# A planner of hand-scheduled steps that repeats its plan, feeds its waits back and counts all DMAs as one pipe

## The chip, the core and the metric

The program runs on one core of a Trainium2 chip. The metric is device time in microseconds (us) from the first to the last instruction, plus a little that lies around that span; the time given is a median of several executions, and a profile is taken of one execution.

## What is computed

Causal attention over two batches of 12 heads (448 positions, head size 64) gives x of 896 rows by 768. Two feed-forward stages follow, and only these are touched by the change:

```python
def _moe_ref(x, w_in, w_out):            # first feed-forward
    h = x @ w_in                         # 896x768 @ 768x2048
    g = h * np.cos(h)
    return (g @ w_out).astype(np.float32)   # 896x2048 @ 2048x768
...
def _moe2_ref(x, w_in, w_out):           # second feed-forward
    h = x @ w_in
    g = np.where(pos, h, np.where(neg, 0.0, (h + beta) ** 2 / (4.0 * beta)))
    return (g @ w_out).astype(np.float32)
```

The weights come as 64-bit floats and are decoded to 32-bit on the core.

## The kernel before

**Stages.** Attention comes first, in an order fixed by a table. Each feed-forward then has a first half (x @ w_in, matmuls of line L645, a few of L517) and a second half (g @ w_out, matmuls of L815). Every product of 32-bit values is made of three matmuls, since both operands are split into a high and a low part: the high part is a cast on ScalarE (ACT), the low part a subtraction on VectorE (DVE).

**The second half uses a seven-product scheme** (fewer block products, more sums): 28 products, numbered t = 0 to 27, seven groups of four, each of three pieces of six matmuls. Before product t its weight side (`wh`, `wl`) and its activation side (`xh`, `xl`) are split. The sums of blocks that the scheme needs are made partly by DMA: an accumulating DMA that POOL issues (L605), called S2, S3, S4 for weights (tile `ws`, 384 KB) and T2, T3, T4 for activations (tile `gs`, 448 KB), each with the block number 0 to 3 behind a dot.

**Loads.** The SP queue issues the weight loads in order: `raw` (L223, w_in, 768 KB in pieces of 1 KB) and `rows` (L730, w_out, 768 KB in pieces of 6 KB). There are two `raw` buffers, shared with the last `rows` of each stage, so the first two loads of the second feed-forward, raw16 and raw17, wait until DVE has decoded the `rows` that lie in their buffers.

**The planner.** All steps of both feed-forwards are registered with `plan.add(name, engine, us, make, after)`: a step's engine, its assumed duration, the function that emits its instructions, and the steps it must follow. Names begin with the stage, 0 or 1. The steps that matter here: `L` load a raw unit, `A` decode it on ACT (L241 and L243, two instructions), `l`, `a`, `k`, `m` the load of a `rows` unit, its words on ACT, its clamp and its bits on DVE (L246, then L262 and L265), `g` a sign change on POOL (L748), `wh`/`xh` the high parts on ACT (L773, L775), `wl`/`xl` the low parts on DVE (L781, L783), `N` a sign change on ACT (L602), `p1` a copy of a finished result bank on ACT (L827), `c` a sum of results on DVE (L838), `D` the products on TensorE (PE, L815).

`Plan.run` gives every step a latest start (`late`), counted back from the PE steps, whose order is fixed. Then it walks through time: each engine takes, of the steps that are ready, the one with the earliest `late`. A step's result counts as usable after a fixed lag, which for anything on SP is 6 us and on POOL 7 us however many DMAs are under way. The order found is the order in which the instructions are emitted, so each engine runs its own queue in that order, and an instruction that waits holds all behind it on its engine.

Of the kernel before, what the change touches and what calls it, by code (L numbers as in the profile page):

```python
# [88 lines left out]
class Plan:  # L89


    LAG = {"PE": 0.1, "ACT": 0.15, "DVE": 0.1, "SP": 6.0, "POOL": 7.0}

    MARGIN = 0.0
# [6 lines left out]
    def add(self, name, engine, us, make, after=(), lag=None):  # L101
        after = [(a, self.ops[a]["lag"]) for a in after if a in self.ops]
        op = dict(engine=engine, us=us, make=make, after=after, lag=self.LAG[engine] if lag is None else lag)
        if engine == "PE":
            if self.last_pe:
                op["after"].append((self.last_pe, 0.0))
            self.last_pe = name
        assert name not in self.ops
        self.ops[name] = op

    def run(self):

        ops = self.ops
        t = self.BUSY["PE"]
        for op in ops.values():
            op["late"] = 1e9
            if op["engine"] == "PE":
                op["late"] = t
                t += op["us"]
        order = list(ops)  # L120
        for name in reversed(self.sorted(order)):
            op = ops[name]
            for a, lag in op["after"]:
                margin = self.MARGIN if op["engine"] == "PE" and ops[a]["engine"] != "PE" else 0.0
                ops[a]["late"] = min(ops[a]["late"], op["late"] - lag - margin - ops[a]["us"])
        free = {e: self.BUSY.get(e, 0.0) for e in self.LAG}
        waiting = {e: [n for n in order if ops[n]["engine"] == e] for e in free}
        self.log = []
        while any(waiting.values()):
            best = None  # L130
            for e, names in waiting.items():
                can = []
                for n in names:
                    if all("end" in ops[a] for a, _ in ops[n]["after"]):
                        r = max([ops[a]["end"] + lag for a, lag in ops[n]["after"]] + [-9.0])
                        can.append((r, n))
                    if e == "PE":
                        break
                if can:
                    start = max(free[e], min(r for r, _ in can))  # L140
                    if best is None or start < best[0]:
                        ready = [n for r, n in can if r <= start]
                        best = (start, e, min(ready, key=lambda n: ops[n]["late"]))
            start, e, n = best
            waiting[e].remove(n)
            ops[n]["start"], ops[n]["end"] = start, start + ops[n]["us"]
            free[e] = ops[n]["end"]
            self.log.append((start, e, n, ops[n]["late"]))
            ops[n]["make"]()

    def sorted(self, order):
        seen, out = set(), []

        def visit(n):
            if n not in seen:
                seen.add(n)
                for a, _ in self.ops[n]["after"]:
                    visit(a)
                out.append(n)

        for n in order:
            visit(n)
        return out

# [2 lines left out]
def attention_then_two_ffn(  # L167
# [436 lines left out]
    def sum_by_dma(to, what):  # L604
        nc.gpsimd.dma_start(out=to, in_=what, accum_op=ALU.add)  # L605
# [11 lines left out]
    OWN = 10  # L617
# [3 lines left out]
    def ffn(k):  # L621
# [5 lines left out]
        XRING, P1, P17, P174 = ((0, 4, 5, 14), (BIG, 14, 5, 4))[k]  # L627
        x = x1 if k == 0 else None

        def add(name, engine, us, make, after=(), lag=None):  # L630
            plan.add(f"{k}{name}", engine, us, make, [a[1:] if a[0] == "@" else f"{k}{a}" for a in after], lag)

        def before(name):
            return ["@0" + name] if k else []
# [224 lines left out]
        def weights(f):  # L859
            u = base + f  # L860
            if (k, f) != (0, 2):
                add(f"A{f}", "ACT", 1.8, partial(decode, u), [f"L{f}"] + ([f"O{f - 2}"] if f > 1 else before(f"O{KF - 2 + f}")))
            add(f"K{f}", "DVE", 0.56, partial(decode, u), [f"A{f}"])
            add(f"M{f}", "DVE", 1.92, partial(decode, u), [f"K{f}"])
            if f + 2 < KF:
                add(f"L{f + 2}", "SP", 0.1, partial(load_unit, u + 2), [f"M{f}", f"L{f + 1}"])
            prior = [f"H{f - 1}"] if f else before(f"wh{NT7 - 1}")
            prior += unit_products(f - 4) if f >= 4 else [a for d in range(ML) for a in before(f"D{NT7 - 4 + f}.{d}")]
            add(f"H{f}", "ACT", 0.82, partial(decode, u), [f"M{f}"] + prior)
            if u in UNIT_LO_BY_DMA:  # L870
                add(f"h{f}", "ACT", 0.82, partial(decode, u), [f"H{f}"])
                add(f"O{f}", "POOL", 1.0, partial(decode, u), [f"h{f}"])
            else:
                add(f"O{f}", "DVE", 0.95, partial(decode, u), [f"H{f}"])

        if k:
            for f in range(2):
                add(f"L{f}", "SP", 0.1, partial(load_unit, base + f), [f"@0m{KF - 2 + f}"] + ([f"L{f - 1}"] if f else []))
            weights(0)
            weights(1)  # L880
        ACC = 0.6045
# [23 lines left out]
        for f in range(0, KF, 2):  # L905
# [14 lines left out]
            for i in (f, f + 1):  # L920
                j, ii, q = spot(i)
                need = unit_products(i) + ([f"X{i - 2}"] if i > 1 else [f"@0c12.{d}" for d in range(ML)] if k else [])
                if k == 0:
                    add(f"G{i}", "ACT", 1.85, partial(start_gate, i), need)
                    add(f"R{i}", "DVE", 1.05, step(gates, i), [f"G{i}"])
                    add(f"S{i}", "ACT", 1.15, step(gates, i), [f"R{i}"])
                    add(f"X{i}", "DVE", 1.05, step(gates, i), [f"S{i}"])
                else:
                    add(f"G{i}", "ACT", 2.95, partial(start_gate, i), need)
                    add(f"X{i}", "DVE", 1.1, step(gates, i), [f"G{i}"])  # L930
                    add(f"N{i}", "ACT", 0.55, step(gates, i), [f"X{i}"])
                if q and ii:
                    add(
                        f"T3.{j}", "POOL", 1.0, partial(lambda j: sum_by_dma(part(j, 1), part(j, 3)), j),
                        [f"X{i - 3}", f"X{i - 2}", f"X{i - 1}", f"X{i}", f"N{i}", f"N{i - 2}"],
                    )
                if i + 2 < KF:
                    weights(i + 2)
# [3 lines left out]
        for n in range(KF):  # L942
# [5 lines left out]
            add(f"l{n}", "SP", 0.1, partial(load_rows, n), ([f"l{n - 1}"] if n else []) + free + ([f"L{KF - 1}"] if n >= OWN else []))  # L948
# [3 lines left out]
            add(f"g{n}", "POOL", 0.65, partial(rows_minus, n), [f"m{n}"], lag=0.15)  # L952
            if i and not q:
                add(f"S3.{j}", "POOL", 1.0, partial(sum_by_dma, ws[j][:, 1], ws[j][:, 0]), [f"g{n - 1}", f"g{n}"])

        def ready_of(n):
            return f"m{n}", f"g{n}"
# [12 lines left out]
        def add_split(t):  # L970
# [6 lines left out]
            add(f"wh{t}", "ACT", 0.82, partial(split_hi, t, "w"), sw + ([f"wh{t - 1}"] if t else []) + [f"H{KF - 1}"] + done(t - 4))  # L977
            if t in by_dma:
                add(f"wm{t}", "ACT", 0.82, partial(split_lo_minus, t), [f"wh{t}"])
                add(f"wl{t}", "POOL", 1.0, partial(split_lo_add, t), [f"wm{t}"])  # L980
# [15 lines left out]
        for t in range(NT7):  # L996
# [12 lines left out]
                        need = [f"{a}{e}" for a in ("wh", "wl", "xh", "xl")] + (free[d // 2] if free else [])  # L1009
                        add(f"D{e}.{d}", "PE", 1.21, partial(product, e, d), need)  # L1010
            if p == 0:
                add(
                    f"T2.{j}", "POOL", 1.0, partial(lambda j: sum_by_dma(part(j, 0), part(j, 1)), j),
                    [f"T3.{j}", f"xh{t}", f"xl{t}"],
                )
            if p == 1:
                add(
                    f"S2.{j}", "POOL", 1.0, partial(sum_by_dma, ws[j][:, 1], ws[j][:, 3]),
                    [f"S3.{j}", f"wh{t}", f"wl{t}"] + odd(j),
                )  # L1020
                add(
# [5 lines left out]
                    [f"S2.{j}", f"wh{t - NJ}", f"wl{t - NJ}"],  # L1027
                )
            if p == 2:
                add(  # L1030
                    f"T4.{j}", "POOL", 1.0, partial(lambda j: sum_by_dma(part(j, 2), part(j, 0)), j),
                    [f"T2.{j}", f"xh{t}", f"xl{t}"],
                )
                add(
                    f"S4.{j}", "POOL", 1.0, partial(sum_by_dma, ws[j][:, 2], ws[j][:, 1]),
                    [f"S2.{j}", f"wh{t}", f"wl{t}"],
                )
            if j == NJ - 1:
# [62 lines left out]
```

## Time and profile before

| | us |
|---|---|
| median of 3 runs | 532.63 (532.59 to 533.18) |
| the profiled execution's own time | 532.24 |
| its span, first to last instruction | 530.4 |
| PE busy in the span | 517.1 (97%) |
| DVE busy | 432.8 (82%) |
| ACT busy | 396.5 (75%) |
| POOL busy | 120.3 (23%) |

The profiled execution lies 0.39 us under the median, and 1.84 us of its time lie around its span. "Idle" of an engine is the time in which it ran no instruction; the profile names what ended each idle stretch.

### The profile page before, as it was taken

To read this page: it belongs to the slowest core of one execution; us is meant where nothing else is said; L and a number is where in the kernel's file an instruction comes from. 1 tells how busy PE (TensorE), PEld (TensorE's weight loads), DVE (VectorE), ACT (ScalarE), POOL (GpSimd) and SP (SyncE) were. 2 spreads that over 40 slices of the span, in tenths; PEclk is the share of its full clock that TensorE was granted. 3 is DMA by queue.
4 is the path that set the end of the run, shared out by engine and by line. 5 is a ranking of instruction groups with operands and counts; after the bars stand their busy time and mean duration, and the time that the engine had idled before them with its cause. 6 is when DMAs were issued, how large, how long until landed. Compare 5 with 4: busy or idle time off the path is not lost.

```text
span 530.4 us, 7822 instructions
## 1 busy us (share of the span) xinstructions
PE 517.1 (97%) x2865; PEld 451.3 (85%) x2865; DVE 432.8 (82%) x589; ACT 396.5 (75%) x634; POOL 120.3 (23%) x178
## 2 busy tenths in 40 slices
PE   7999999999999999997999999999999999999996
PEld 3677668898989899896989999898989898999996
DVE  6878797999998989993997896879887489986751
ACT  5999856998988869862845677999989998655430
POOL 2766562203111112460000001011101235400000
PEclk9999999999999999999999999999999999999999
DMA  8741116957787346999030258577863779960111
GB/s 313 261 122 41 41 61 210 303 173 210 246 244 230 91 122 142 210 210 231 1 107 13 74 175 258 179 208 234 225 197 82 160 140 231 197 138 0 53 52 53
DMA packets 43702, 82.68 MB, mean 156 GB/s; under 512 B 2576, under 2 KB 31888, under 8 KB 43664
## 3 DMA queue, kind: packets, MB, share of 16 engines
q1 hardware_dynamic: 36464, 61.40, 35.4%
q0 software_dynamic: 6912, 20.45, 20.8%
q8 instruction: 22, 0.36, 0.3%
q10 hardware_dynamic: 288, 0.34, 0.2%
q14 instruction: 16, 0.13, 0.1%
HBM read 58.98 MB, written 2.75 MB: 116 GB/s over the span
## 4 chain that ended last, share of the span: by engine, by line
PE 85%; DVE 7%; DMA 4%; ACT 3%; issue 1%; DVEq 0%; ACTq 0%
PE m L645 41%; PE m L815 30%; PE o L466 4%; DMA raw<-in_moe_w_in 4%; PE m L517 2%; PE sa L352 2%; PE tx L441 2%; PE sb L352 1%; DVE s L781 1%; DVE slo L781 1%; PE sc L337 1%; PE tw L441 1%; PE warm L545 1%; PE tz L441 1%; DVE nma L380 1%
## 5 line engine op out<-in xcount | busy, mean ns | idle before, releaser
L645 PE MATMUL m<-x,whi 128*128 128x512 f32 (+2 forms) x728 | 204.8, 362 | 0.0
L815 PE MATMUL m<-s,shi 128*128 128x448 f32 x648 | 185.6, 368 | 4.2 <-ACT shi L773 3.3
L645 PEld LDWEIGHTS m<-x,whi 128*128 128x128 f32 x728 | 134.4, 188 | 14.2
L815 PEld LDWEIGHTS m<-s,shi 128*128 128x128 f32 x648 | 122.2, 189 | 15.4 <-ACT shi L773 3.7
L645 PE MATMUL m<-x,wlo 128*128 128x512 f32 (+2 forms) x364 | 131.9, 362 | 0.0
L815 PE MATMUL m<-s,slo 128*128 128x448 f32 x324 | 119.0, 367 | 0.0
L748 POOL TENSOR_SCALAR ws<-ws 128x384 f32<-128x384 f32 x32 | 25.9, 811 | 236.6 <-DVE ws L265 121.7
L645 PEld LDWEIGHTS m<-x,wlo 128*128 128x128 f32 x364 | 68.3, 188 | 7.0
L815 PEld LDWEIGHTS m<-s,slo 128*128 128x128 f32 x324 | 61.2, 189 | 5.4 <-DVE slo L781 0.5
L781 DVE TENSOR_TENSOR slo<-ws,shi 128x768 fp32r<-128x768 f32 x56 | 54.0, 967 | 9.5 <-ACT shi L773 9.5
L773 ACT CAST shi<-ws 128x768 fp32r<-128x768 f32 x56 | 46.1, 827 | 2.1 <-issue 1.8
L775 ACT ACTIVATE s<-gs 128x896 fp32r<-128x896 f32 x30 | 28.5, 948 | 19.1 <-PE m L815 15.5
L241 ACT ACTIVATE f<-raw 128x768 f32<-128x768 f32 x32 | 28.9, 906 | 15.0 <-DMA raw<-in_moe_w_in 13.7
L783 DVE SCALAR_TENSOR_TENSOR s<-gs,s 128x896 fp32r<-128x896 f32 x30 | 33.2, 1107 | 6.9 <-ACT s L775 6.8
L773 ACT CAST s<-gs 128x896 fp32r<-128x896 f32 x24 | 22.7, 945 | 20.4 <-PE m L815 20.3
L716 DVE TENSOR_TENSOR gs<-m,ax 128x896 f32<-128x896 f32 x16 | 17.5, 1091 | 22.6 <-ACT ax L714 18.8
L605 POOL DMA_DIRECT2D gs<-gs x24 | 23.3, 972 | 48.9 <-DVE s L783 14.1
L781 DVE TENSOR_TENSOR s<-gs,s 128x896 fp32r<-128x896 f32 x24 | 26.4, 1100 | 7.2 <-ACT s L773 7.1
L265 DVE SCALAR_TENSOR_TENSOR ws<-ws,rows 128x768 uint32<-128x768 uint32 x32 | 30.9, 964 | 1.1
L296 DVE TENSOR_TENSOR wlo<-f,whi 128x768 fp32r<-128x768 f32 x30 | 28.8, 960 | 3.4 <-ACT whi L287 3.4
L241 ACT ACTIVATE ws<-rows 128x768 f32<-128x768 f32 x32 | 29.1, 911 | 2.8 <-DMA rows<-in_moe_w_out 2.6
L262 DVE SCALAR_TENSOR_TENSOR rows<-rows 128x768 uint32<-128x768 uint32 x32 | 30.5, 953 | 0.3 <-ACT rows L243 0.2
(104 smaller groups left out, 799.9 us busy)
## 6 DMA issues: line engine op xcount, KB each, us to landing
raw<-in_moe_w_in SPq DMA_DIRECT2D x32, 768.0 KB, 4.7
rows<-in_moe_w_out SPq DMA_DIRECT2D x32, 768.0 KB, 5.2
gs<-gs POOLq DMA_DIRECT2D x24, 448.0 KB, 5.7
ws<-ws POOLq DMA_DIRECT2D x24, 384.0 KB, 6.9
v<-in_v SPq DMA_DIRECT2D x12, 256.0 KB, 2.7
k<-in_k SPq DMA_DIRECT2D x12, 224.0 KB, 3.9
qr<-in_q SPq DMA_DIRECT2D x11, 224.0 KB, 4.4
out<-c SPq DMA_DIRECT2D x11, 224.0 KB, 2.0
```

What stands on the lines that cost most here:

```text
L241: nc.scalar.activation(out=fl, in_=high.bitcast(F32), func=AF.Abs, scale=UP)
L262: nc.vector.scalar_tensor_tensor(out=low, in0=high, scalar=0x80000000, in1=low, op0=ALU.bitwise_and, op1=ALU.bitwise_or,)
L265: nc.vector.scalar_tensor_tensor(out=bits, in0=bits, scalar=3, in1=low, op0=ALU.logical_shift_left, op1=ALU.bitwise_or,)
L296: e.tensor_tensor(out=lo[:, :m], in0=fl, in1=f32(hi)[:, :m], op=ALU.subtract)
L605: nc.gpsimd.dma_start(out=to, in_=what, accum_op=ALU.add)
L645: nc.tensor.matmul(o, w[a][:, c, :], x_of(t, c)[:, s], start=(c == first and n == 0), stop=(c == last and n == 2),)
L748: nc.gpsimd.tensor_scalar(out=t, in0=t, scalar1=-1.0, scalar2=1.0, op0=ALU.mult, op1=ALU.mult)
L773: nc.scalar.copy(out=hi, in_=src)
L775: nc.scalar.mul(out=hi, in_=src, mul=-1.0)
L781: nc.vector.tensor_tensor(out=lo, in0=src, in1=f32(hi), op=ALU.subtract)
L783: nc.vector.scalar_tensor_tensor(out=lo, in0=src, scalar=-1.0, in1=f32(hi), op0=ALU.mult, op1=ALU.subtract)
L815: nc.tensor.matmul(o, l[:, i, d * P : (d + 1) * P], r[:, i], start=(p in (0, 2, 4) and j == 0 and i == 0 and n == 0), stop=(j == NJ - 1 an ...
```

## The change

Only the planner and the way in which steps describe their DMAs change. No step is added or removed and no dependency changes, so the same instructions run. The PE order is fixed, as before.

- A step that issues a DMA (`add_load`, `add_sum`) now carries the DMA's share of one common pipe (2.4 us for a load, 2.3 us for a sum). In the model DMAs leave this pipe one after the other, a DMA lands 2.6 us after it left, and a step is not issued while the pipe is more than 3 us behind.
- Durations of ACT, DVE and POOL steps are raised by 1.5 to 2%.
- `run` now plans up to 200 times. Of the best plan so far it picks one wait of PE, follows it back through what it waited for, and either makes the steps on the way more urgent (`early`) or holds one step back (`held`); a plan that ends no later is kept.

```diff
-    LAG = {"PE": 0.1, "ACT": 0.15, "DVE": 0.1, "SP": 6.0, "POOL": 7.0}
+    LAG = {"PE": 0.1, "ACT": 0.15, "DVE": 0.1, "SP": 0.1, "POOL": 0.15}
+    PACE = {"PE": 1.0, "ACT": 1.015, "DVE": 1.015, "SP": 1.0, "POOL": 1.02}
+    DMA_PACE = 1.1
+    LANDING = 2.6
+    BACKLOG = 3.0
     BUSY = {"PE": 11.8, "DVE": 1.3, "ACT": 1.5, "POOL": 0.6}
+    ROUNDS = 200
...
+    def once(self, early, held):
...
+                ready = [(max(r, pipe - self.BACKLOG) if ops[n]["dma"] else r, n, why) for r, why, n in steps]
...
+            r, n, why = min((x for x in ready if x[0] <= start), key=lambda x: ops[x[1]]["late"] - early.get(x[1], 0.0))
...
+            if op["dma"]:
+                pipe = end = max(pipe, free[e]) + op["pipe"]
...
+    def run(self):
+        self.wanted()
+        draw = random.Random(1)
+        early, held, best = {}, {}, None
+        for _ in range(self.ROUNDS):
+            end, log, waits, behind = self.once(early, held)
+            if best is None or end <= best[0]:
+                best = (end, log, waits, behind, early, held)
+            end, log, waits, behind, early, held = best
+            if not waits:
+                break
+            early, held = dict(early), dict(held)
+            wait, n = draw.choice(waits)
+            step = (wait + 1.0) * draw.uniform(-0.5, 3.0)
+            hold = draw.random() < 0.5
+            for _ in range(draw.randrange(1, 16)):
+                r, n, before = behind[n]
+                if n is None:
+                    break
+                if not hold:
+                    early[n] = early.get(n, 0.0) + step
+            if hold and n and behind[n][2]:
+                held[behind[n][2]] = behind[n][0]
+        self.log = best[1]
+        for _, _, n, _ in self.log:
+            self.ops[n]["make"]()
...
+        def add_load(name, make, after):
+            add(name, "SP", 0.1, make, after, 2.4)
+
+        def add_sum(name, make, after):
+            add(name, "POOL", 1.0, make, after, 2.3)
...
-                add(f"L{f + 2}", "SP", 0.1, partial(load_unit, u + 2), [f"M{f}", f"L{f + 1}"])
+                add_load(f"L{f + 2}", partial(load_unit, u + 2), [f"M{f}", f"L{f + 1}"])
```

**What moves.** The order differs in many places on ACT, DVE and POOL and in a few on SP. Three of them are shown, the rows of before first and those of the change behind (line numbers of the change are some 64 to 70 higher).

POOL, second half of the first feed-forward, from the sum S2.2 (tile ws2) to the last sum S4.3 (ws3); a `gs..0` that writes gs0..1 is a T4:

```order
L605 DMA ws2_1378<-ws2_1378 128x768
L605 DMA gs001_1461<-gs000_1435 128x896
L605 DMA ws0_1376<-ws0_1376 128x768
L605 DMA gs011_1708<-gs010_1677 128x896
L605 DMA ws1_1377<-ws1_1377 128x768
L605 DMA gs021_1956<-gs020_1929 128x896
L748 TENSOR_SCALAR ws3_1379<-ws3_1379 128x384
L605 DMA ws2_1378<-ws2_1378 128x768
L748 TENSOR_SCALAR ws3_1379<-ws3_1379 128x384
L605 DMA ws3_1379<-ws3_1379 128x768
L605 DMA gs031_2196<-gs030_2161 128x896
L605 DMA ws3_1379<-ws3_1379 128x768
```

```order
L669 DMA ws2_1378<-ws2_1378 128x768
L669 DMA gs001_1470<-gs000_1435 128x896
L669 DMA gs011_1709<-gs010_1673 128x896
L669 DMA ws0_1376<-ws0_1376 128x768
L818 TENSOR_SCALAR ws3_1379<-ws3_1379 128x384
L669 DMA gs021_1948<-gs020_1914 128x896
L818 TENSOR_SCALAR ws3_1379<-ws3_1379 128x384
L669 DMA gs031_2193<-gs030_2156 128x896
L669 DMA ws3_1379<-ws3_1379 128x768
L669 DMA ws1_1377<-ws1_1377 128x768
L669 DMA ws2_1378<-ws2_1378 128x768
L669 DMA ws3_1379<-ws3_1379 128x768
```

The sums S4.1 (ws1) and S4.2 (ws2) stood before the second sign change (g15) and now stand behind it, after T4.3 and S2.3.

DVE, the same stretch, around the decoding of rows014, which frees the buffer that raw16 is loaded into (`slo` is a `wl`, `s` an `xl`, `L246 ... ws3` a `k`):

```order
L781 TENSOR_TENSOR slo08_2463<-ws0_1376,shi08_2462 128x768
L781 TENSOR_TENSOR s09_2494<-gs011_1708,s09_2494 128x896
L781 TENSOR_TENSOR slo09_2505<-ws1_1377,shi09_2504 128x768
L246 TENSOR_SCALAR ws3_1379<-ws3_1379 128x2x384
L781 TENSOR_TENSOR s010_2522<-gs021_1956,s010_2522 128x896
L262 SCALAR_TENSOR_TENSOR rows014_2427<-rows014_2427 128x768
L265 SCALAR_TENSOR_TENSOR ws3_1379<-ws3_1379,rows014_2427 128x2x384
```

```order
L851 TENSOR_TENSOR slo08_2468<-ws0_1376,shi08_2467 128x768
L672 TENSOR_TENSOR ws0_1376<-ws0_1376 128x768
L310 TENSOR_SCALAR ws3_1379<-ws3_1379 128x2x384
L851 TENSOR_TENSOR s09_2502<-gs011_1709,s09_2502 128x896
L851 TENSOR_TENSOR slo09_2507<-ws1_1377,shi09_2506 128x768
L326 SCALAR_TENSOR_TENSOR rows014_2421<-rows014_2421 128x768
L329 SCALAR_TENSOR_TENSOR ws3_1379<-ws3_1379,rows014_2421 128x2x384
```

The clamp of rows014 now stands ahead of xl9 and wl9, and its bits directly behind wl9, ahead of xl10; a sum on DVE (S1.0) has moved ahead of it.

On ACT the decoding of raw16 (f16, step 1A0) stays where it was, between wh12 and wh13; that of raw17 moves from behind wh14 to behind wh16.

ACT, second half of the second feed-forward, from the split xh4 (`s14`) on; `gs131_...<-gs131_...` is a sign change, the last one N15, on which the sum T3.3 (to gs130) waits, and `p11` are the copies `p1`:

```order
L775 ACTIVATE s14_4148<-gs100_3255 128x896
L773 CAST shi14_4157<-ws0_1376 128x768
L602 ACTIVATE gs131_4001<-gs131_4001 128x448
L241 ACTIVATE ws2_1378<-rows112_3974 128x2x384
L243 ACTIVATE rows112_3974<-rows112_3974 128x768
L775 ACTIVATE s15_4186<-gs110_3487 128x896
L773 CAST shi15_4197<-ws1_1377 128x768
L827 COPY p11_4200<-m37_4089 128x448
L775 ACTIVATE s16_4208<-gs120_3730 128x896
L827 COPY p11_4200<-m37_4089 128x448
```

```order
L845 ACTIVATE s14_4155<-gs100_3256 128x896
L843 CAST shi14_4164<-ws0_1376 128x768
L666 ACTIVATE gs121_3760<-gs121_3760 128x448
L845 ACTIVATE s15_4177<-gs110_3486 128x896
L843 CAST shi15_4187<-ws1_1377 128x768
L897 COPY p11_4198<-m37_4084 128x448
L666 ACTIVATE gs131_3997<-gs131_3997 128x448
L897 COPY p11_4198<-m37_4084 128x448
L666 ACTIVATE gs131_3997<-gs131_3997 128x448
L897 COPY p11_4198<-m38_4085 128x448
```

N15 stood two splits ahead of `p1.0` and now follows `p1.1`.

## Rows read from the trace of the kernel before

**Rows 1.** Waits of PE from 95 us on: who waited, total us, times, longest us

```profile
PE m L815 <- ACT shi L773: 3.3, 1, 3.3
PE m L815 <- DVE c L838: 0.4, 1, 0.4
PE m L815 <- ACT p L827: 0.4, 2, 0.2
```

**Rows 2.** Timeline of PE where product 13 begins: start, us, what, idle before

```profile
250.86 1.11 PE L815 MATMUL m<-s,shi 128*128 128x448 f32 x2 [3.31 <-ACT shi L773]
```

**Rows 3.** Timeline of ACT, 237 to 250 us

```profile
248.44 0.89 ACT L241 ACTIVATE f<-raw 128x768 f32<-128x768 f32 x1 [9.66 <-DMA raw<-in_moe_w_in]
```

**Rows 4.** The chain that ended last: start, us, what

```profile
199.38 12.41 PE m L815 x60
...
229.71 18.70 DMA raw<-in_moe_w_in
...
308.12 115.66 PE m L645 x576
423.79 13.39 PE m L815 x66
...
438.62 87.84 PE m L815 x432
```

**Rows 5.** Stretch: us, busy PE PEld DVE ACT POOL, PEclk, DMA share, GB/s

```profile
247.00:256.00 9.00, 5.69 (x20) 4.49 (x19) 4.59 (x6) 7.56 (x10) 0.85 (x1) 0.81 0.49 127
```

**Rows 6.** DMA queues from 234 to 246 us: packets, MB, share of 16 engines

```profile
q0 software_dynamic: 673, 1.98, 85.0%
q1 hardware_dynamic: 737, 0.75, 22.1%
```

**Rows 7.** DMA queues and issues from 74 to 79 us, no sum under way

```profile
q1 hardware_dynamic: 784, 0.79, 50.9%
...
raw<-in_moe_w_in SPq DMA_DIRECT2D x2, 768.0 KB, 4.6
```

**Rows 8.** Timeline of POOL, sums issued around raw16's load

```profile
223.25 0.86 POOL L605 DMA_DIRECT2D ws<-ws  x1 [0.30 <-POOL ws L748]
...
228.07 0.86 POOL L605 DMA_DIRECT2D gs<-gs  x1 [0.44 <-DVE s L781]
...
230.83 0.86 POOL L605 DMA_DIRECT2D ws<-ws  x1
234.12 1.28 POOL L748 TENSOR_SCALAR ws<-ws 128x384 f32<-128x384 f32 x1 [2.43 <-DVE ws L265]
235.70 0.88 POOL L605 DMA_DIRECT2D ws<-ws  x1 [0.30 <-POOL ws L748]
236.27 1.18 POOL L605 DMA_DIRECT2D gs<-gs  x1
```

**Rows 9.** DMA issues from 223.2 to 223.3 us: KB each, us to landing

```profile
ws<-ws POOLq DMA_DIRECT2D x1, 384.0 KB, 6.9
```

**Rows 10.** DMA issues from 228 to 229 us

```profile
gs<-gs POOLq DMA_DIRECT2D x1, 448.0 KB, 13.9
```

**Rows 11.** Timeline of DVE, 224 to 230 us

```profile
224.16 1.09 DVE L781 TENSOR_TENSOR s<-gs,s 128x896 fp32r<-128x896 f32 x1 [0.40 <-ACT s L773]
...
226.04 0.55 DVE L246 TENSOR_SCALAR ws<-ws 128x768 f32<-128x768 f32 x1
...
227.69 0.95 DVE L262 SCALAR_TENSOR_TENSOR rows<-rows 128x768 uint32<-128x768 uint32 x1
```

**Rows 12.** Waits of PE before 95 us

```profile
PE sb L352 <- ACT p L402: 1.5, 2, 1.4
```

**Rows 13.** Timeline of ACT, second feed-forward: p1.1 and xh7

```profile
438.06 0.51 ACT L827 COPY p<-m 128x448 f32<-128x448 f32 x1
...
441.27 0.94 ACT L775 ACTIVATE s<-gs 128x896 fp32r<-128x896 f32 x1
```

**Rows 14.** DMA issues from 447 to 468 us

```profile
gs<-gs POOLq DMA_DIRECT2D x4, 448.0 KB, 8.9
```

More of the change, by code (lines that the diff above doesn't have):

```diff
@@ L1 @@
 import math
+import random
 import struct
@@ L109, in add, with lag, wanted @@
         self.ops[name] = op
-    def run(self):
-        ops = self.ops
+    def lag(self, a, op):
+        return 0.0 if a["engine"] == op["engine"] == "PE" else a["lag"]
+    def wanted(self):
         t = self.BUSY["PE"]
-        for op in ops.values():
+        for op in self.ops.values():
             op["late"] = 1e9
@@ L118, in run @@
                 op["late"] = t
[L119 to L125, printed above, removed]
+                t += op["time"]
+        for name in reversed(self.sorted()):
+            op = self.ops[name]
+            for a in (self.ops[n] for n in op["after"]):
+                a["late"] = min(a["late"], op["late"] - self.lag(a, op) - a["pipe"] - a["time"])
@@ L126, in run @@
+    def once(self, early, held):
+        ops = self.ops
+        need = {n: len(op["after"]) for n, op in ops.items()}
+        then = {n: [] for n in ops}
+        for n, op in ops.items():
+            for a in op["after"]:
+                then[a].append(n)
+        can = {e: [] for e in self.LAG}
+        for n in need:
+            if not need[n]:
+                can[ops[n]["engine"]].append((-9.0, None, n))
         free = {e: self.BUSY.get(e, 0.0) for e in self.LAG}
-        waiting = {e: [n for n in order if ops[n]["engine"] == e] for e in free}
@@ L128, in run @@
-        self.log = []
-        while any(waiting.values()):
+        last = dict.fromkeys(free)
+        pipe = 0.0
+        done, behind, log, waits = {}, {}, [], []
+        while len(log) < len(ops):
             best = None
[L131 to L149, printed above, removed]
@@ L151, in sorted @@
-    def sorted(self, order):
+            for e, steps in can.items():
+                if not steps:
+                    continue
+                ready = [(max(r, pipe - self.BACKLOG) if ops[n]["dma"] else r, n, why) for r, why, n in steps]
+                start = max(free[e], min(ready)[0])
+                if best is None or start < best[0]:
+                    best = (start, e, ready)
+            start, e, ready = best
+            r, n, why = min((x for x in ready if x[0] <= start), key=lambda x: ops[x[1]]["late"] - early.get(x[1], 0.0))
@@ new lines, in once @@
+            op = ops[n]
+            can[e] = [x for x in can[e] if x[2] != n]
+            behind[n] = (r, why, last[e])
+            last[e] = n
+            if e == "PE" and start > free[e]:
+                waits.append((start - free[e], n))
+            free[e] = start + op["time"]
+            end = free[e]
+            if op["dma"]:
+                pipe = end = max(pipe, free[e]) + op["pipe"]
+            done[n] = end
+            log.append((start, e, n, op["late"]))
+            for m in then[n]:
+                need[m] -= 1
+                if not need[m]:
+                    r, why = max((done[a] + self.lag(ops[a], ops[m]), a) for a in ops[m]["after"])
+                    can[ops[m]["engine"]].append((max(r, held.get(m, r)), why, m))
@@ L152, in sorted @@
+    def sorted(self):
         seen, out = set(), []
@@ L156, in visit @@
                 seen.add(n)
-                for a, _ in self.ops[n]["after"]:
+                for a in self.ops[n]["after"]:
                     visit(a)
                 out.append(n)
-        for n in order:
+        for n in self.ops:
             visit(n)
```

44 lines of the change are left out of this document (21 added, 23 removed).

## The prediction

> **What bounds the kernel now.** The page gives PE 97% of the span, and no step's work changes, so the first view to read is who made PE wait. From the end of attention on there are three kinds of wait: one of 3.3 us for the cast `shi` on ACT, two of 0.2 us for the copies `p`, one of 0.4 us for a sum `c` [rows 1]. The long one stands at 247.55 to 250.86 us, where product 13 of the first feed-forward should begin [rows 2]. The reader should next ask why ACT was late with that cast. It had no work of its own to finish: it sat idle for 9.66 us, until 248.44, in front of the decoding of raw16, and wh13 is queued right behind that decoding [rows 3]. The chain of waits names the same culprit, a load issued at 229.71 that took 18.70 us [rows 4], where the same kind of load takes 4.6 us when no sum is under way [rows 7].
>
> Why so long? While PE ran up to the stop, the queue of the sums moved 673 packets and the queue of the loads 737 in the same 12 us [rows 6]. The two queues take turns about packet by packet. A raw load consists of 784 packets [rows 7], small ones (1 KB pieces), and each waits for a far larger packet of a sum. At 737 per 12 us, 784 packets take 12.8 us; the other 5.9 us of the 18.70 lie before its first packet and behind its last. So the load is slow for as long as sums are queued.
>
> How much is there to win? Both feed-forwards run the same 504 matmuls of L815. The first does so from 199.38 to 308.12, in 108.74 us; the second from 423.79 to 438.62 + 87.84 = 526.46, in 102.67 us [rows 4]. The first loses 6.07 us more than the second. Each also has one wait of 0.2 us for `p` [rows 1], so waits in the products cost 6.07 + 0.4 = 6.5 us in all. Of these, 3.3 and 0.4 are the named idle times, and 1.7 is the clock: over the 9.00 us from 247 the granted clock is 0.81 on average, that is 2 x 0.19 x 9.00 = 3.4 us at 1.2 instead of 2.4 GHz, half of it lost [rows 5]. It fell after PE had stood still for 3.31 us. The rest, 0.7 us, I put to restarts. Everything else on PE is matmuls back to back, and the change neither shortens nor removes one.
>
> **The change part by part.** Nothing is added or removed; the planner runs before the program is built and costs nothing on the chip. The larger durations and the pipe in its model cost nothing by themselves either, they only pick the order. The price of the change is therefore what the new order does to the 6.5 us, and whether it makes a new wait.
>
> First, the load of raw16. It waits for the bits of rows014 on DVE. Those now follow wl9 directly. In the trace xl9 starts at 224.16, since it waits for ACT (0.40 us idle), then comes wl9, then the clamp at 226.04, one more split, and the bits at 227.69 [rows 11]. With the clamp and that split out of the way the bits can start at 226.04, 1.65 us earlier. (The clamp and S1.0 must then fit ahead of 224.16; T1.1, a sum of some 1.1 us on DVE, was moved behind, which makes the room.) So the load is issued 1.65 us earlier, near 228.1.
>
> Second, the sums around it. From 223.25 to 228.07 POOL issued six, which stood ahead of the load, one more at 230.83, and the next at 235.70 and 236.27, behind a sign change that ends at 235.40 [rows 8]. The first of the six landed at 223.25 + 6.9 = 230.15 [rows 9], the sixth at 228.07 + 13.9 = 241.97 [rows 10]: 2.36 us for each of the five between. In the new order S4.1 and S4.2 leave this place and go behind the sign change, T4.3 and S2.3. Five sums stand ahead of the load, and the last of them, T4.2, should land near 239.6. T4.3 is held by the sign change until about 235.4, so by these rows it joins some 4 us before the queue is empty, and the load keeps taking turns with sums to its end, as before.
>
> Third, what follows. If the load takes as long as it did, it lands 1.65 us earlier, and so does everything queued behind it on ACT (wh13, then wl13 on DVE). PE itself arrives 0.2 us earlier, without its first wait for `p`. The stop at product 13 shrinks from 3.31 to 3.31 - 1.65 + 0.2 = 1.9 us. Whether the clock falls after 1.9 us is not in the trace. It was kept after 1.4 us in attention [rows 12] and lost after 3.31; 1.9 is nearer to the first, so I take 0, and 1.7 as the upper end.
>
> Fourth, the two waits for `p` and that for `c`. The first two come from work that ACT does between the copies p1.0 and p1.1, a decoding in the first feed-forward, the split xh6 in the second; the decoding now stands ahead of both, and a shorter sign change has taken the split's place. The third was DVE's lateness after the long stop, which shrinks. I count all three as gone; 0.8 us is what they cost if none is.
>
> Fifth, the many other moves (sums and sign changes later in the second feed-forward, loads one or two places up or down). Their cover is the lead with which splits run ahead of PE; I cost them at nothing and take the tightest as a rival below.
>
> Sum: without any wait in the products, 532.24 - 6.5 for the profiled execution, 526.1 against the median of 532.63, which lies 0.39 us above. With 1.9 us left at product 13: **528.0 us**.
>
> **The rivals.** *No stop at all.* The sum S2.2 is held by a sign change behind the bits of rows013, and these move ahead of four DVE steps (two `wl`, an `xl` and the sum T1.1, each of about 1 us, as the steps of [rows 11]), so the five sums may start up to some 4 us earlier, and T4.2's packets may be through when T4.3 arrives near 235.4. Then raw16's packets have the pipe to themselves, 784 in 4.6 us instead of 12.8 [rows 7]. The stop vanishes if the load lands 1.9 us sooner than I forecast. For it speaks that a gap of 1 us moves about a fifth of the load, against it the 4 us of queue by the rows above. Time 526.1.
>
> The Trainium skill, page "DMA: Bandwidth & Descriptors", section "Queues, rings and completion order", says that an engine goes round its queues and takes some 9 to 17 descriptors from one before it switches. By that rule a raw load would pass in a few turns, the stop would not be there, and the time would come out as this rival's, 526.1. The trace does not agree: 673 packets to 737 in the same stretch [rows 6] are turns of about one to one, so the page adds little to this rival's chance.
>
> *The change does not do what it says there.* The pipe is full until all sums of this stretch are through, and as many bytes are asked for as before. If raw16 gets through only at the end of that crowd, it lands as late as before, the stop stays at 3.5 us and the clock falls. Then only the small waits go, 0.8 us: 531.8.
>
> *Slower.* In the second feed-forward T3.3 now waits for N15 behind `p1.1`. That copy ends at 438.57, and a sign change is short (the xh beside it takes 0.94), so T3.3 is issued near 439.1. Product 7 begins three products after 438.62: 54 matmuls of 87.84 / 432 = 0.203 us [rows 4], at 449.6. Ahead of it lie xh7, 0.94 us [rows 13], and xl7, 1.09 us [rows 11]. T3.3 may thus take 8.4 us. In the crowd of that stage such sums took 8.9 us [rows 14], but few stand ahead of T3.3. If it takes 13.9 us, as one did in the first feed-forward [rows 10], PE stops for 5.5 us there and loses 1.7 of clock: 535.2. It makes the kernel slower, on top of my forecast, from a landing of about 12.4 us on.
>
> **How the numbers follow.** Forecast, a shortened stop: 0.43, of which 0.13 with a fallen clock (529.7). No stop: 0.37. As late as before: 0.12. Slower: 0.08. A run of this kernel can tell about 0.2% from no change, 1.1 us. The first two cases are faster, and a little of the third: 0.85. The rest of the third and mild forms of the fourth are within 0.2%: 0.09. Slower: 0.06. The range reaches from the no-stop case less the uncertainty of the restarts (526.1 - 0.7 = 525.4) to a stop left at its full 3.3 us with the clock's 1.7 us (526.1 + 5.0 = 531.1), which leaves out the last two cases.
>
> **What would show it.** Right: the wait of PE for the cast `shi` at product 13 is 1 to 3 us; ACT's idle time in front of raw16's decoding is shorter than 9.66 us but still the longest; the load is issued 1 to 2 us earlier and takes over 12 us; the two waits for `p` are gone; the second feed-forward's products take 102 to 102.7 us. The first rival shows as a load of under 15 us and no wait of PE over 0.5 us; the second as a landing at 248 us or later; the third as a wait of PE for xh or xl at products 6 or 7 of the second feed-forward. Wrong altogether would be a new wait in the first halves (L645), where the trace of before has none.

## The result, and the profile after

The changed kernel takes 527.99 us (median of 4 runs, 527.64 to 528.06) beside 532.61 for the kernel before (4 runs): a ratio of 0.9913, interval 0.9896 to 0.9930. The forecast was 528.0. The way there was another than the forecast's, though: two of its steps were wrong by about 2 us each, in opposite directions.

The profiled execution took 527.64 us. From the end of attention on, its list of PE's waits is empty; the stop of 3.3 us and the three short ones [rows 1] are gone. The chain of waits (start, us, what) is therefore PE alone:

```profile
199.53 104.16 PE m L885 x504
303.68 115.93 PE m L715 x576
419.61 102.16 PE m L885 x504
```

To be read against [rows 4]: the first feed-forward's 504 products take 104.16 us instead of 108.74, the second's 102.16 instead of 102.67. But neither waits any more, so why do the same 504 matmuls take 2.00 us more in the first?

The load of raw16, first by DMA issues and queues (KB, us to landing; then packets, MB, share), from 228 to 229, from 228 to 232, from 232 to 236 and from 233 to 234 us:

```profile
raw<-in_moe_w_in SPq DMA_DIRECT2D x1, 768.0 KB, 8.2
...
q0 software_dynamic: 244, 0.75, 102.6%
q1 hardware_dynamic: 64, 0.07, 6.0%
...
q1 hardware_dynamic: 720, 0.72, 54.1%
q0 software_dynamic: 122, 0.37, 50.7%
...
q1 hardware_dynamic: 327, 0.33, 99.9%
q0 software_dynamic: 5, 0.01, 3.3%
```

It was issued at 228.13 us, as forecast, but took 8.2 us, not 18.7. Its first packet moved at 230.26, and up to 232 us it took turns with the sums. Then there was a hole in their packets: the last of S4.0 started at 233.14, the first of T4.2 at 234.33, and in the 1 us from 233 the load moved 327 packets and the sums 5. In the kernel before, raw16 met no such hole from its first packet at 233.59 up to 246 us; a small one at 241 is all there is. From 234 to 241 us the turns were one to one, in total as shown and nearly so in each single us:

```profile
q0 software_dynamic: 393, 1.17, 86.6%
q1 hardware_dynamic: 387, 0.40, 20.5%
```

What was sent out around the hole is seen on POOL (timeline: start, us, what, idle before), to be compared with [rows 8], and on DVE, with [rows 11]:

```profile
219.61 0.86 POOL L669 DMA_DIRECT2D ws<-ws  x1 [0.30 <-POOL ws L818]
...
226.16 1.18 POOL L669 DMA_DIRECT2D ws<-ws  x1
228.15 1.28 POOL L818 TENSOR_SCALAR ws<-ws 128x384 f32<-128x384 f32 x1 [0.82 <-DVE ws L329]
229.38 0.86 POOL L669 DMA_DIRECT2D gs<-gs  x1
234.67 1.27 POOL L818 TENSOR_SCALAR ws<-ws 128x384 f32<-128x384 f32 x1 [4.43 <-DVE ws L329]
235.90 0.87 POOL L669 DMA_DIRECT2D gs<-gs  x1
```

```profile
217.11 0.96 DVE L329 SCALAR_TENSOR_TENSOR ws<-ws,rows 128x768 uint32<-128x768 uint32 x1
...
223.78 0.55 DVE L310 TENSOR_SCALAR ws<-ws 128x768 f32<-128x768 f32 x1
...
226.12 0.94 DVE L326 SCALAR_TENSOR_TENSOR rows<-rows 128x768 uint32<-128x768 uint32 x1
```

S2.2 is issued at 219.61 instead of 223.25, since the bits of rows013 end at 218.07. Where before sent out six sums in 4.8 us, S4.0 (226.16) is now followed by a sign change, T4.2 goes out 3.2 us behind it at 229.38, and T4.3 only at 235.90, held by the second sign change. Between the packets of S4.0 and T4.2 lies the hole in which raw16 came through; between those of T4.2 and T4.3, near 238 us, lies another, in which raw17, issued at 234.63, came through in 6.2 us. T4.2's first packet moved 4.95 us after its issue, though a sum issued with none in flight takes 1.4 us (208.51 us in before); why it was so late is open. On ACT the decoding of raw16 no longer shows an idle time in front of it (9.66 us in [rows 3]); it runs 2.8 us behind the landing:

```profile
239.08 0.91 ACT L305 ACTIVATE f<-raw 128x768 f32<-128x768 f32 x1
```

The clock is kept. The stretch of [rows 5] (us, busy time of PE, PEld, DVE, ACT, POOL, then the granted clock) now reads:

```profile
247.00:256.00 9.00, 9.00 (x46) 8.16 (x45) 7.36 (x10) 5.62 (x7) 0.00 (x0) 1.00 0.23 43
```

There remains the pace. Stretches of before, then of after, PE alone, at a clock of 1.00 in all:

```profile
202.00:212.00 10.00, 10.00 (x50) 1.00 0.72 133
216.00:246.00 30.00, 30.00 (x150) 1.00 1.01 218
440.00:500.00 60.00, 60.00 (x298) 1.00 0.57 124
```

```profile
216.00:246.00 30.00, 30.00 (x147) 1.00 1.06 246
260.00:290.00 30.00, 30.00 (x147) 1.00 0.17 54
440.00:500.00 60.00, 60.00 (x298) 1.00 0.58 123
```

PE is busy throughout, but does 150 matmuls in 30 us before and 147 after. From start to start a 448-column matmul takes either 0.2027 us on average or, evenly, 0.2067. Before began the products at 0.2067 (12.41 us for 60, [rows 4]) and ran at 0.2027 from its short wait for `p` near 214.5 us on. After, which waits for nothing, stayed at 0.2067 until those matmuls ended near 318 us. Whether that wait had done it was the second question for the experiments; what frees the load was the first.

### The profile page after: what moved, and what is told of

Same layout as the page of the kernel before. It is cut to its first block, busy times and chain, and to the rows that moved or that the text cites. A ratio compares the mean times of both kernels' runs of the same rounds, so it can differ in the third digit from the quotient of the medians.

```text
span 525.8 us, 7812 instructions
## 1 busy us (share of the span) xinstructions
PE 516.5 (98%) x2865; PEld 450.4 (86%) x2865; DVE 433.7 (82%) x589; ACT 397.2 (76%) x634; POOL 120.5 (23%) x178
## 4 chain that ended last, share of the span: by engine, by line
PE 95%; DVE 3%; ACT 1%; issue 0%; DVEq 0%
PE m L715 42%; PE m L885 39%; PE o L530 4%; PE m L581 2%; PE sa L416 2%; PE tx L505 2%; PE sb L416 1%; PE sc L401 1%; PE tw L505 1%; PE tz L505 1%; DVE nma L444 1%; PE warm L609 1%; ACT p L466 1%; DVE f L319 0%; DVE pT L517 0%
## 5 line engine op out<-in xcount | busy, mean ns | idle before, releaser
L818 POOL TENSOR_SCALAR ws<-ws 128x384 f32<-128x384 f32 x32 | 27.9, 872 | 243.2 <-DVE ws L329 131.8
L669 POOL DMA_DIRECT2D gs<-gs x24 | 22.1, 930 | 49.8 <-ACT gs L666 11.1
```

What stands on the lines that cost most here:

```text
L818: nc.gpsimd.tensor_scalar(out=t, in0=t, scalar1=-1.0, scalar2=1.0, op0=ALU.mult, op1=ALU.mult)
```

## The experiments

In all but the planner's and the split ones a short list moves steps behind the order that the planner found; ("a", "b") puts step a directly behind b on its engine, everything else keeps its order. Each ratio is to runs of before taken beside that kernel (their medians lie between 532.61 and 533.72 us). Attention ends up to 2.3 us later in these profiles than in before's, so the table gives raw16's load from the first product on (its row in the chain, 199.38 us in before).

| kernel | load issued | landed | S2.2 issued | PE's longest wait behind attention | ratio to before (interval) |
|---|---|---|---|---|---|
| before | 30.33 | 49.03 | 23.87 | 3.3 | 1 |
| after | 28.60 | 36.76 | 20.08 | none | 0.9913 (0.9896 to 0.9930) |
| bits earlier | 28.81 | 48.47 | 23.85 | 2.8 | 1.0000 (0.9986 to 1.0014) |
| sums earlier | 30.31 | 43.56 | 20.37 | 1.8, another place | 0.9947 (0.9925 to 0.9968) |
| POOL's order | 30.32 | 41.79 | 23.85 | 1.9, another place | 0.9990 (0.9972 to 1.0008) |
| ACT later | 30.30 | 49.09 | 23.85 | 0.2 | 0.9885 (0.9865 to 0.9904) |
| after, POOL's old order | 28.62 | 42.00 | 20.09 | none | 0.9909 (0.9888 to 0.9929) |
| feedback without pipe | 28.69 | 47.74 | 21.62 | 9.3 | 1.0093 (1.0072 to 1.0115) |

**Bits earlier: the forecast's own mechanism, alone.**

```diff
+MOVES = (("0k14", "0wl8"), ("0m14", "0wl9"))
```

> The kernel before, with the clamp and the bits of rows014 moved up on DVE as the change has them, and all sums as before. By the prediction (the load takes turns with sums from its issue on) raw16 is issued 1.65 us earlier, lands near 246.8, the stop at product 13 is 1.5 to 2 us and the time 528.5 to 531. By the rival (the load moves only once the sums ahead of it are out) it is issued earlier but lands within 0.7 us of 248.4, the stop stays at 2.7 to 3.4 us and the time at 531.5 to 533.

The load is issued 1.5 us earlier and lands 0.6 us earlier; the time does not change. The rival's landing and stop came out: an earlier issue buys next to nothing as long as the sums leave no hole (663 packets of the load to 693 of the sums from 233 to 245 us). Two things besides the load's issue changed: T4.2, whose split on DVE now stands behind these bits, went out 1.3 us later than in before, and behind the stop the products ran at 0.2067 us instead of 0.2027, an estimated 1.1 us for 268 of them, which hides the 0.5 us by which the stop is shorter.

**Sums earlier, alone.**

```diff
+MOVES = (("0m13", "0xl6"), ("0T1.1", "0wl10"))
```

> The kernel before, with the bits of rows013 moved up on DVE behind xl6 and the sum T1.1 moved behind wl10 as the change has them, so that the DMA sums from S2.2 on start up to 3.5 us earlier; their order on POOL is as before. If it is the emptying of the sums' queue that frees the load, raw16 takes well under 15 us, lands before 245, the stop is under 1 us and the time 526.5 to 528.5. If the load's own issue sets its landing, it lands near 247.3 (T1.1 gone from ahead of it, 1.1 us), the stop is 2 us or more and the time 530 to 532.

The load is issued as late as before, but lands 5.5 us earlier, and product 13 no longer stops. The turns are one to one here too, until the sums sent out ahead of the second sign change are through: from 241 to 242 us the load moves 360 packets and they 6. The gain is cut by a second stop of 1.8 us, which ends at 276.14 us, for a sum `c` of DVE. DVE is late there because ACT stands still once more, now for raw17, whose decoding this kernel still has behind wh14 (ACT, then DVE):

```profile
249.76 0.91 ACT L241 ACTIVATE f<-raw 128x768 f32<-128x768 f32 x1 [2.38 <-DMA raw<-in_moe_w_in]
...
252.20 0.96 DVE L781 TENSOR_TENSOR slo<-ws,shi 128x768 fp32r<-128x768 f32 x1 [3.00 <-ACT shi L773]
```

Behind this stop the clock fell (stretch and busy times as in [rows 5], then the granted clock). A wait of 0.4 us ahead of it, at 268.30, had already brought the matmuls from 0.2027 to 0.2067 us:

```profile
276.00:285.00 9.00, 8.86 (x36) 8.09 (x37) 7.19 (x9) 4.35 (x7) 0.00 (x0) 0.81 0.04 14
```

**POOL's order, alone.**

```diff
+MOVES = (("0T4.1", "0T4.0"), ("0g14", "0S4.0"), ("0T4.3", "0g15"), ("0S4.1", "0S2.3"), ("0S4.2", "0S4.1"))
```

> The kernel before, with only POOL's order of the last eight sums of the first feed-forward taken from the change (S4.1 and S4.2 behind the second sign change, T4.3 and S2.3). If the order of the sums alone frees the load, raw16 lands before 244 and the stop is gone: 526.5. If the sums have to start earlier as well, T4.3 still joins near 236 before the five ahead are out, raw16 lands at 246 or later, the stop is 1.5 to 3.3 us and the time 529 to 532.5.

A miss on the load: it lands 7.2 us earlier with nothing started earlier. S4.1 and S4.2 are out of its way, and T4.2, now behind the first sign change, goes out 2.8 us later than in before; the load comes through in two holes, in the us from 236 and from 240 (packets, MB, share):

```profile
q1 hardware_dynamic: 228, 0.23, 76.8%
q0 software_dynamic: 14, 0.03, 16.0%
...
q1 hardware_dynamic: 266, 0.27, 77.4%
q0 software_dynamic: 21, 0.05, 24.0%
```

In the second of them five sums were issued and not yet landed, so what counts is not how many sums are in flight but whether their packets are there. The time is unchanged all the same, since raw17 took the stop over: PE's waits there, of 0.4 to 1.9 us, come to 3.8 us, and from 278 to 286 us, behind the longest, the granted clock is 0.79. raw17 needed 17.59 us, and ACT idled 6.51 us for it:

```profile
252.51 0.89 ACT L241 ACTIVATE f<-raw 128x768 f32<-128x768 f32 x1 [6.51 <-DMA raw<-in_moe_w_in]
```

**The sums earlier and raw17's decoding later.**

```diff
+MOVES = (("0m13", "0xl6"), ("0T1.1", "0wl10"), ("1A1", "0wh16"))
```

> The kernel before, with three steps moved: the bits of rows013 up on DVE, T1.1 behind wl10 (both as in the run that starts the sums earlier) and raw17's decoding on ACT from behind wh14 to behind wh16, where the change has it. If the second stop of that run (1.8 us for the sum c, with DVE idle 3 us for shi behind raw17's decoding) came from the place of raw17's decoding, it goes: raw16 takes 13 to 14 us, PE stops for neither, ratio to before 0.986 to 0.990. If it came from T1.1 standing late on DVE, the wait for c stays and the ratio is 0.994 to 0.996.

The profiled execution has neither stop, only the waits for `p`, so the second stop did come from the place of raw17's decoding. raw16 took 13.4 us. The ratio is 0.9935 (0.9906 to 0.9963), short of what was expected. The profiled execution took 528.74 us, as much as the median, and its chain shows where the rest lies:

```profile
201.70 12.41 PE m L815 x60
...
435.16 87.83 PE m L815 x432
```

From the first product to the end of the last that is 321.29 us, 5.8 less than in before (327.08), as much as was expected of the moves; but attention, of which they touch no step, ended 2.3 us later. Of the other nine runs, 526.9 to 533.8 us, there is no trace.

**ACT later: leave the load late and take wh13 out from behind it.**

```diff
+MOVES = (("1A0", "0wh16"), ("1A1", "1A0"))
```

> The kernel before, with one thing moved: ACT decodes raw16 and raw17 only behind wh16 instead of between wh12 and wh13. If the stop at product 13 came only from wh13 standing behind a decoding that waits for its load, the load still lands near 248.4 us but PE does not stop: 532.6 less 3.3 (stop), 1.7 (clock), 0.7 (restarts) and 0.4 (wait for c) gives 526.5 us. If the late load holds up something else as well (DVE's decoding, a buffer, the first half of the second feed-forward), a new wait appears behind it and the time stays above 529. On the pace of the products: if a short wait of PE at product 4 is what brings the 448-column matmuls from 0.207 to 0.203 us each, they stay at 0.203 here, since that wait stays; if it was the long stop, they run at 0.207 up to the end of this half and the time is near 528.5.

The load takes 18.8 us as ever, and nobody minds. With two steps moved on one engine the kernel before gains as much as with the whole change (527.68 us, 4 runs). What waits are left:

```profile
PE m L815 <- ACT p L827: 0.4, 2, 0.2
PE m L815 <- DVE c L838: 0.2, 1, 0.2
```

The matmuls came down to 0.2027 us at product 4 here too, without any long stop.

**The change with POOL's old order.**

```diff
+MOVES = (("0S4.0", "0T4.0"), ("0T4.1", "0S4.0"), ("0S4.1", "0T4.1"), ("0T4.2", "0S4.1"), ("0g14", "0T4.2"), ("0S4.2", "0g14"), ("0g15", "0S4.2"), ("0S2.3", "0g15"), ("0T4.3", "0S2.3"), ("0S4.3", "0T4.3"))
```

> The changed kernel, with POOL's order of the last sums of the first feed-forward taken from before (S4.1 and S4.2 ahead again), the rest as changed: the sums start as early as changed, but one more stands ahead of raw16's load. If the early start is what counts, raw16 takes 10 to 14 us, lands before 243, product 13 does not stop and the ratio to before stays at 0.990 to 0.993. If the order of the sums is needed too, it lands behind 245, PE stops 1 us or more at product 13 and the ratio is 0.995 or more.

The load takes 13.4 us instead of 8.2, and PE waits no more than in the changed kernel. So the new order of the sums makes a hole for the load, but is not needed once they start earlier.

**Which half of the planner?** One round of planning, so the pipe without the feedback, and the feedback with the old lags, so without the pipe:

```diff
-    ROUNDS = 200
+    ROUNDS = 1
```

> The changed kernel with one round of planning instead of 200: the pipe and the larger durations act, the feedback does not. Its order on ACT has raw16's decoding behind wh14 and its T4 sums stand together. The planner's model then sees PE wait 10.5 us in all (0.8 at product 4 and 1.9 at product 20 of the first, 7.8 at product 11 of the second feed-forward) where it sees 3.7 with feedback. If the model is right in that, the kernel is about 6.8 us slower than the changed one, ratio near 1.004; if it sees waits that are not there, the order is as good and the ratio 0.988 to 0.993.

```diff
-        op["pipe"] = dma * self.DMA_PACE
-        op["lag"] = self.LANDING if dma else self.LAG[engine]
+        op["pipe"] = 0.0
+        op["lag"] = {"SP": 6.0, "POOL": 7.0}[engine] if dma else self.LAG[engine]
```

> The changed kernel, with the planner's old lags (6 us for a load, 7 us for a sum) in place of the common pipe; 200 rounds of feedback and the larger durations stay. Its order has the early bits on DVE, but S4.1 ahead of T4.2, and raw16's decoding stands ahead of wh11 and wh12. If the pipe in the model is needed, the load lands near 243 (as with POOL's old order, 13 us), wh11 comes some 4 us too late for product 11 near 241, PE stops, the clock falls and the ratio is 0.998 or more. If feedback alone does it, the load lands near 236 and the ratio is 0.986 to 0.992.

Each half alone is slower than before: 1.0037 (1.0022 to 1.0052) and 1.0093. Both keep the larger durations (a sign change `g` went from 0.65 to 0.75 us), which were not tried alone, and each stands for the one plan that its search found. With one round PE waits 5.7 us: 0.2 at product 4 and 1.6 at product 20 of the first feed-forward, and the rest in the second, for `shi` and then `slo`, where that planner's model also had its longest wait (PE's timeline):

```profile
463.03 0.68 PE L885 MATMUL m<-s,shi 128*128 128x448 f32 x2 [2.28 <-ACT shi L843]
465.35 0.74 PE L885 MATMUL m<-s,slo 128*128 128x448 f32 x1 [1.64 <-DVE slo L851]
```

Without the pipe the planner puts raw16's decoding ahead of wh11, and the sums leave the load no hole. It takes 19.0 us, ACT idles 13.30 for it, and PE stops 9.3 us (queues from 234 to 246 us, then ACT):

```profile
q0 software_dynamic: 685, 2.01, 86.0%
q1 hardware_dynamic: 691, 0.71, 21.0%
...
248.86 0.89 ACT L305 ACTIVATE f<-raw 128x768 f32<-128x768 f32 x1 [13.30 <-DMA raw<-in_moe_w_in]
```

**A wait put back.** In the changed kernel:

```diff
+MOVES = (("0a13", "0p1.0"),)
```

> The changed kernel, with one step moved: on ACT the words of rows013 go between the copies p1.0 and p1.1, where the kernel before has them, so that PE should again wait some 0.2 us for p1.1 at product 4 of the first feed-forward. If a short wait re-sets the pace of the matmuls, those behind it take 0.2027 instead of 0.2067 us up to the end of the 448-column ones near 318 us: about 500 times 0.004 us is 2.0 us, less 0.2 to 0.4 us of wait, so 1.6 to 1.8 us faster than the changed kernel, ratio to before near 0.988. If the pace hangs on something else (the order of other work, the load of memory), it stays at 0.2067, the wait is added and the ratio is 0.991 to 0.992.

526.63 us (4 runs), ratio 0.9872 (0.9851 to 0.9894): a kernel that waits is faster than the one that does not. In its profile PE waits 0.17 us at product 4, and the 432 matmuls behind it take 87.82 us, 0.2033 each, where the 60 in front take 0.2068 (PE's timeline, then the chain):

```profile
214.99 0.67 PE L885 MATMUL m<-s,shi 128*128 128x448 f32 x2 [0.17 <-ACT p L897]
...
199.94 12.41 PE m L885 x60
214.99 87.82 PE m L885 x432
...
418.46 102.16 PE m L885 x504
```

From the first product to the end of the last that is 418.46 + 102.16 - 199.94 = 320.68 us, against 419.61 + 102.16 - 199.53 = 322.24 in the changed kernel: 1.56 less, of the 1.6 to 1.8 expected.

**No wait, but a break in the rhythm.** One matmul of the 504, done as two:

```diff
+                    first = (k, t, d, i, n) == (0, 0, 0, 0, 1)
+                    for c in (slice(0, 256), slice(256, S)) if first else (slice(0, S),):
-                        o, l[:, i, d * P : (d + 1) * P], r[:, i],
+                            o[:, c], l[:, i, d * P : (d + 1) * P], r[:, i, c],
```

> The changed kernel, with the second matmul of product 0 of the first feed-forward done as two, of 256 and 192 columns: PE never waits, but everything behind is shifted against the clock by an odd amount. If only an idle PE re-sets the pace, all stays at 0.2067 us and the ratio to before is 0.991 to 0.992. If any break in the even stream of matmuls draws the pace anew, it may fall to 0.2027 from product 0 on (504 and some 60 more matmuls, 2.2 us): ratio near 0.987, with one chance in two.

525.72 us (4 runs), ratio 0.9851 (0.9830 to 0.9872), the fastest of all, below both kernels. The extra matmul costs nothing that can be seen, and the products take 102.18 us from the first on:

```profile
200.08 102.18 PE m L887 x505
...
417.92 102.16 PE m L887 x504
```

So an idle PE is not needed; a break is enough. Which way does a break go? The same split in both feed-forwards:

```diff
-                    first = (k, t, d, i, n) == (0, 0, 0, 0, 1)
+                    first = (t, d, i, n) == (0, 0, 0, 1)
```

> The changed kernel with the second matmul of product 0 done as 256 and 192 columns in both feed-forwards; the second had the pace of 0.2027 us already. If the split leads to the faster pace whatever went before, both halves take 102.2 us and the time is that of the split in the first alone, 525.7. If each break draws the pace anew, the second may fall to 0.2067, 104.2 us there, and the time is near 527.7.

```profile
200.03 102.18 PE m L887 x505
...
417.87 104.19 PE m L887 x505
```

The second half, at 0.2027 us in the profiles of all thirteen other kernels, is now the slow one (527.93 us, one run). A break can thus lead either way, and it need not change anything: the wait for `p` near 438 us in before left 0.2027 as it was.

```diff
-                    for c in (slice(0, 256), slice(256, S)) if first else (slice(0, S),):
+                    for c in (slice(0, 320), slice(320, S)) if first else (slice(0, S),):
```

> The changed kernel with the second matmul of product 0 of the first feed-forward done as 320 and 128 columns instead of 256 and 192. If any split leads to the faster pace, the products take 102.2 us and the time is 525.7; if the pace hangs on the exact shift, they may stay at 104.2 us, 527.9.

526.87 us in one run, with the products at 102.20 us: the faster pace again, so it does not hang on whether the matmul is cut at 256 or at 320 columns. Attention ended about 1 us later than in the 256-column run.

## Why the time was right and the reasons only in part

- **What bounds the kernel: right.** The late load cost PE through ACT's queue, where wh13 stood behind a decoding that waited. Moving that decoding alone took the stop away while the load stayed late.
- **The issue of raw16 at 228.1: right** (228.13), and so were T4.2's landing (239.6 forecast, 238.45 measured) and T4.3's issue (235.4 and 235.90).
- **"The load keeps taking turns with sums to its end", and with it "if the load takes as long as it did": the first step that failed.** The turns were right: in before, and in the runs above until a hole came, the packets of raw16 and of the sums went one to one. But the forecast laid the sums end to end at 2.36 us each and carried the 18.70 us over whole from a queue of six sums, soon seven, to a shorter one. There the packets of S4.0 were through and those of T4.2 had not begun when the load's turn came, and it took 8.2 us. The load lands when it meets a hole, not some time after its issue; the runs with only the issue, only the sums' start and only their order changed tell the three apart. The stop left over, forecast at 1.9 us, was none.
- **The first rival: right in its signs and in part of its reason.** The load took under 15 us, PE waited for nothing, and the sums started up to 4 us earlier (3.6 measured). But it looked for the hole behind T4.2, and the load was through ahead of it. A gap of 1 us moved 327 of its 784 packets, not a fifth.
- The Trainium skill, page "DMA: Bandwidth & Descriptors", section "Queues, rings and completion order", whose 9 to 17 descriptors a turn stood beside that rival, is not borne out. Turns of equal length, however long, give counts of one to one, so [rows 6] could not settle it, and by such turns the load would still stand behind as many packets of the sums as it has itself: "a few turns" and a stop that is gone do not follow from the rule. The starts of the packets settle it: from 234.5 to 240.5 us of before, a sum's packet starts 50 to 75 ns behind some four in five of the load's 334 (about 60 ns long each) beyond what chance gives, and no second one of the load's. These are turns of one.
- **The clock after a stop of 1.9 us, put at nothing: not borne out, though the changed kernel did not come to it.** Behind the stops of 1.8 us (sums earlier) and 1.9 us (POOL's order) the granted clock was 0.81 and 0.79 on average, where shorter waits of 0.4 to 0.8 us stood some 6 us ahead of either. With the forecast's stop and this clock the time would have been its own 529.7.
- **"Everything else on PE is matmuls back to back, and the change neither shortens nor removes one": the second step that failed, by 2.3 us.** The sum without waits, 526.1, took the faster pace for granted. It counted the 0.2 us wait at product 4 as a loss; with it went the break after which the products ran at 0.2027. The first feed-forward's products cost 104.16 - 102.16 = 2.00 us more, and the first matmuls of the next half 115.93 - 115.66 = 0.27.
- **Why the time agrees.** From the first product to the end of the last, before takes 438.62 + 87.84 - 199.38 = 327.08 us, the changed kernel 322.24, the split kernel, with no wait and the faster pace, 417.92 + 102.16 - 200.08 = 320.00. All that could be had was thus 7.1 us where the forecast counted 6.5. It took 1.9 off for a stop that did not come; the pace took 2.2. That leaves 4.6 and 4.8, and the agreement is luck.
- **The waits for `p` and `c`, the kept clock, the second feed-forward at 102 to 102.7 us: right** (none, 1.00, 102.16). The slower rival, T3.3 late behind N15, did not come: there is no wait at its products 6 and 7.
- **"The planner itself costs nothing, it only picks the order": right**, but pipe and feedback gain only together.

Open: why the matmuls have two paces, and what decides which of them follows a break; and why the packets of T4.2 began so late.

## What to carry to other kernels

A transfer's duration belongs to the queue that it meets, so do not carry it over to an order in which that queue is another. Count the packets of both queues in each us: here they took strict turns, and what set the load's landing was the next hole in the other queue's packets. Before fighting over a transfer's speed, look whether an instruction that waits for it can simply stand later in its engine's queue. And where an engine is busy 100% of a stretch, count its instructions there: here a PE that was busy throughout did 147 matmuls in 30 us in one stretch and 150 in another.

## What the runs showed of the hardware

With one matmul behind the other and a granted clock of 1.00, a 448-column matmul takes either 0.2067 us from start to start, evenly, or 0.2027 on average. The pace holds for hundreds of matmuls and can change at breaks: a wait of 0.17 us, a matmul of another width, or a long stop (the clock fell after both, but after that of the bits-earlier run the products went on at 0.2067, after that of before at 0.2027). In all the runs without a split the first feed-forward's products began at 0.2067. In the first halves (L645) 384 columns take 0.173 us and 512 take 0.227 (medians, before), 0.42 ns for each column more, which is one cycle at 2.4 GHz; 448 such cycles are 0.1867 us, so 16 or 20 ns are lost per matmul. The Trainium skill, page "TensorE: Matmul & The Clock Gate", section "Wait — 56ns, not 53.3ns?", states about 2.5 ns per matmul for its case, by which a 448-column one would take an estimated 0.189 us; no run here shows that, and the measurement decides.

A load in pieces of 1 KB on SP's queue and sums in pieces of 3 or 3.5 KB on POOL's take turns packet by packet (387 to 393 in 7 us of before), about 55 of the load's packets per us, whether two or six sums are in flight. With hardly any of the sums' packets the load moves 327 in 1 us.
